# Start of a fused FFT and MLP kernel: batch 0's x loaded ahead of the small loads, its first transform cut into row halves, weight pieces split earlier

## The chip, the cores and the metric

The kernel runs on one core of a Trainium2 chip. The metric is the device time of one execution in microseconds; lower is better.

## The reference

```python
def _attn_ref(x, w_r, w_i, b_r, b_i):            # x: 8 batches of 3008 x 256
    X = np.fft.rfft(x, axis=1)
    Yr = Xr @ w_r - Xi @ w_i + b_r;  Yi = Xr @ w_i + Xi @ w_r + b_i
    Yr, Yi = (sign(Y) * max(|Y| - 0.01, 0) for Y in (Yr, Yi))
    return np.fft.irfft(Yr + 1j * Yi, n=3008, axis=1)
def _moe_ref(x, w_in, w_out):                     # 24064 x 256, w_in 256 x 2048
    h = x @ w_in
    return (h * np.cos(h)) @ w_out
```

`w_in` and `w_out` are stored as 64-bit floats.

## The kernel before

The FFT of 3008 = 64 x 47 points is done by matmuls. For batch 0 all of it stands in a prologue, in which nothing of the MLP runs yet. **Stage A** (`stage_a0`) is the transform of length 64: six tiles `x0` (128 x 1024, 512 KB each) come from memory, and each block of 128 columns of them is the stationary operand of a matmul that streams the 128 columns of `ff`. These 128 columns hold two 64-row transforms on the diagonal, so half of what is multiplied is zero. A float32 matmul is two instructions on TensorE; the stage has 48 matmuls, 96 instructions. Twelve PSUM banks are copied out to `a0`, ScalarE and VectorE in turn (L435). **Stage B** (`first()` in `stage_b`) transposes (`pq`, L542), transforms along 47 (`pb`, L642), mixes by the weights (`pw`, L664), shrinks, transposes back (`pt`) and transforms back (`pi`, L791). It is a generator; the prologue's loop counts its steps in `i`. Then `stage_c` transforms back along 64 (`pc`) and yields the first MLP tile, t=0 of batch 0, whose matmuls are `ph` (L939 to L941) and `po` (L921 to L925). The MLP's steps are in a fixed order, with later batches' transforms between them.

The **weight pieces** are beside that: 16 pieces of `w_in` and `w_out` come as raw words (`raw`, 512 KB each, issued by GpSimd, L257) and `split_f64` turns each into a high and a low part, with two ScalarE and seven VectorE instructions (L270 to L279, and L332 by `rest`). `W_AT` lists the steps `i` at which a piece enters the order; twelve pieces are split ahead of t=0 (`W_BEFORE`), four in its steps `W_LATE`. Raw loads from index `W_NEXT` on wait for the first `pc` matmul. `split_fourier_w` casts the Fourier weights `ws` to `wf` for later batches (ScalarE L233, VectorE L234). `bounds` prepares the clamp's limits from the biases `bb`; `sig` and `fi` serve the inverse transform; `iw`, `sgn`, `fq` serve later batches; `xt` are batch 1's first two x tiles.

`tc.issue_after(ins)` keeps what is issued under it behind `ins` in the planned order. Each engine runs its own queue in order. The planner sets the order of each queue from its own estimates.

Of the kernel before, what the change touches and what calls it, by code (L numbers as in the profile page):

```python
# [31 lines left out]
XP_BUFS = 6  # L32
W_AT = (8, 16, 24, 32, 40, 48, 56, 64, 74)
W_ORDER = tuple(range(16))
W_EARLY = 10
W_NEXT = 13
W_BEFORE = 12
W_LATE = (0, 3, 6, 9)
W_AHEAD = 3
# [139 lines left out]
def tile_body(ctx: ExitStack, tc, x, w_r, w_i, b_r, b_i, w_in, w_out,  # L179
# [27 lines left out]
    def load_constants():  # L207
        with nc.allow_non_contiguous_dma(reason="bias"):
            for r, bsrc in enumerate((b_r, b_i)):
                nc.gpsimd.dma_start(bb[:, r, :], bsrc.rearrange("(c p) -> p c", p=128))  # L210
        ws["sig"] = pool["pro"].tile([96, 32], F32, name="sig", bufs=1)
        nc.gpsimd.dma_start(ws["sig"], c_sig)
        nc.gpsimd.dma_start(fi[0], c_if)
        ws["minus"] = wk.tile([128, 64], F32, tag="xe", name="minus", bufs=2)
        nc.gpsimd.tensor_scalar(out=ws["minus"], in0=ff[:, 256:], scalar1=-1.0, scalar2=None, op0=ALU.mult)

    def load_split_constants():
        nc.gpsimd.dma_start(iw, c_iw)
        nc.gpsimd.dma_start(sgn.rearrange("p s k -> p (s k)"), c_sgn.bitcast(BF16))
        nc.gpsimd.memset(odd, 0.0)  # L220
# [34 lines left out]
    def load_f64(raw, src, behind_it="x0"):  # L255
        with tc.issue_after(mark[behind_it].ins):
            ins = nc.gpsimd.dma_start(raw if len(src.shape) == 2 else raw.rearrange("p (f e) -> p f e", f=2), src)  # L257
            if behind_it == "pc":
                behind(ins, mark["pc"].ins, "first tile")
        return raw  # L260

    def split_f64(k, hi, lo, raw):
# [16 lines left out]
        nc.scalar.copy(hi, a)  # L279
        rest(lo, a, hi)  # L280

# [134 lines left out]
    def stage_a0():  # L416

        a0[0] = pool["a0"].tile([128, 2, 24, 128], F32, name="a0", bufs=1)
        xs = []
        for c in range(6):  # L420
            xs.append(pool["pro"].tile([128, 1024], F32, tag="xp", name="x0", bufs=XP_BUFS))
            nc.sync.dma_start(xs[c], x[0, :, 1024 * c:1024 * (c + 1)])
        load_f0(0)
        load_f0(1)
        load_fourier_w()
        load_f0(2)
        landed("x0", xs[5][:, :1])
        for n in range(12):
            p = fps("pa")
            for c in range(2):  # L430
                for i in range(2):
                    o, k = 256 * c + 128 * i, 512 * (n % 2) + 256 * i + 128 * c
                    mm(p[:, o:o + 128], xs[n // 2][:, k:k + 128], ff[:, :128], start=o == 0, stop=o == 384,
                       skip_group_check=True)
            mark["dve"] = mark["a0", n % 2] = (nc.vector.tensor_copy if n % 2 else nc.scalar.copy)(  # L435
                a0[0][:, :, 2 * n:2 * n + 2], p.rearrange("p (c i k) -> p c i k", c=2, i=2))

    def stage_a(b):
# [3 lines left out]
        def load(c):  # L442
            if c < 6:
                ld[c] = wk.tile([128, 2, 2, 256], F32, tag="xt", name="xt", bufs=2)
                with tc.issue_after(mark["f0", 2].ins) if b == 1 else ExitStack():
                    ins = (nc.sync if b == 1 else nc.gpsimd).dma_start(
                        ld[c].rearrange("p i g d -> p (i g d)"), x[b, :, 1024 * c:1024 * (c + 1)])
# [84 lines left out]
    def stage_b(b):  # L532
# [15 lines left out]
        def load(q):  # L548
            if b and q < 4:
                fq = wk.tile([128, 512], F32, tag="fq", name="fq", bufs=2)  # L550
                with tc.issue_after(mark["x0"].ins) if b == 1 else ExitStack():
                    loads = [nc.gpsimd.dma_start(fq, c_fq[:, 512 * q:512 * q + 512])]
# [321 lines left out]
    def stage_c(b, t):  # L874
# [23 lines left out]
        for g in range(2):  # L898
            pv = p[g].rearrange("p (c i m) -> p c i m", c=2, i=4)
            thv, tlv = (a.rearrange("p c (i g m) -> p g c i m", i=4, g=2)[:, g] for a in (th, tl))  # L900
            nc.scalar.copy(thv, pv)  # L901
            ins = nc.vector.tensor_tensor(out=tlv, in0=pv, in1=thv.bitcast(F32), op=ALU.subtract)  # L902
            drained(p[g], ins)
        if first:
            with tc.issue_after(ins.ins):
                split_fourier_w()
            mark["yf"] = ins
# [62 lines left out]
    with ExitStack() as first:  # L970
# [13 lines left out]
        fi[0] = pool["pro"].tile([96, 2, 96], F32, name="fi", bufs=1)  # L984
        stage_a0()
        load_constants()
        stages["a"] = stage_a(1)
        side_a = stages["a"].alone()
        next(side_a)
        split = 0  # L990
        stages[0] = stage_b(0)
        for i, _ in enumerate(stages[0].first()):
            if i == 0:
                load_pieces(2)
                with tc.issue_after(mark["x0"].ins):
                    load_split_constants()
            if i == 4:
                with tc.issue_after(mark["a0", 1].ins):
                    sum_fourier_w()
                    bounds()  # L1000
            if split < len(W_AT) and i >= W_AT[split]:
                next(mw)
                split += 1
        for _ in side_a:
            pass
        last, mark["yf"] = mark["yf"], mark["yf0"]
        next(mw)
        mark["yf"] = last
        for _ in range(len(W_AT) + 1, W_BEFORE):
            next(mw)  # L1010
# [101 lines left out]
```

## Time and profile before

| | us |
|---|---|
| median of 3 runs | 2602.94 (2596.9 to 2603.41) |
| the profiled execution | 2602.17 |
| its span | 2600.4 |
| TensorE busy | 2561.9 |
| granted TensorE clock, mean share | 0.995 |

The span runs from the first to the last instruction of the profiled execution; 1.8 us of its time lie around it. Times inside are counted from the start of the span. TensorE's busy share is of instructions in flight, not of its peak.

### The profile page before, as it was taken

How to read it: one execution, taken by the hardware profiler on the slowest of the kernel's cores; microseconds unless marked ns; L12 is line 12 of the kernel's file. 1: busy time of each engine (PE TensorE's matmuls, PEld its weight loads, DVE VectorE, ACT ScalarE, POOL GpSimd, SP SyncE). 2: the span in 40 equal slices, each digit the busy share in tenths (PEclk: the TensorE clock that was granted, in tenths of full speed). 3: DMA queues.
4: the chain of work that ended last, by engine and by line, in shares of the span. 5: the costliest groups of instructions: out<-in, count | busy, mean ns of one | idle time of the engine just before them, and what ended most of it. 6: DMA issues, size and time to landing. Idle time of an engine off the chain costs nothing.

```text
span 2600.4 us, 42935 instructions
## 1 busy us (share of the span) xinstructions
PE 2561.9 (99%) x15961; PEld 2070.0 (80%) x15961; DVE 1937.1 (74%) x3089; ACT 1629.6 (63%) x3003; POOL 977.5 (38%) x946
## 2 busy tenths in 40 slices
PE   8899999999999999999999999999999999999999
PEld 7478778877788777887788877887778888888888
DVE  5887776877768787687777877678776778766665
ACT  5665556655675666655666666666666666666666
POOL 2025452444325443344533455234432333322222
PEclk9999999999999999999999999999999999999999
DMA  7546434444333444254432644235433344210000
GB/s 233 160 116 160 143 107 112 113 143 130 104 95 100 140 131 117 81 141 121 142 93 83 160 139 121 78 103 146 135 105 100 84 111 119 62 46 24 17 25 16
DMA packets 172953, 283.11 MB, mean 109 GB/s; under 512 B 15608, under 2 KB 114200, under 8 KB 169160
## 3 DMA queue, kind: packets, MB, share of 16 engines
q1 hardware_dynamic: 161896, 243.78, 33.3%
q0 software_dynamic: 10112, 35.53, 4.4%
q8 instruction: 126, 2.06, 0.3%
q10 hardware_dynamic: 736, 1.05, 0.1%
q14 instruction: 83, 0.68, 0.1%
HBM read 149.76 MB, written 130.55 MB: 108 GB/s over the span
## 4 chain that ended last, share of the span: by engine, by line
PE 87%; DVE 6%; DMA 3%; ACT 2%; issue 1%; SPq 0%; POOL 0%; DVEq 0%; ACTq 0%; POOLq 0%
PE ph L939 12%; PE po L921 12%; PE ph L940 12%; PE ph L941 12%; PE po L925 12%; PE po L922 12%; PE pw L668 2%; PE pw L669 2%; PE pw L670 2%; PE pc L381 1%; PE pb L381 1%; PE pw L664 1%; DVE u L952 1%; DVE u L949 1%; DVE Xl L332 1%
## 5 line engine op out<-in xcount | busy, mean ns | idle before, releaser
L329 POOL TENSOR_TENSOR gl<-u,gh 128x512 fp32r<-128x512 f32 (+1 forms) x384 | 500.7, 1304 | 1125.6 <-ACT gh L954 942.6
L951 ACT ACTIVATE u<-u 128x512 f32<-128x512 f32 (+1 forms) x768 | 478.0, 623 | 385.7 <-DVE u L949 384.8
L952 DVE TENSOR_TENSOR u<-ph,u 128x512 f32<-128x512 f32 (+1 forms) x768 | 518.0, 675 | 236.3 <-ACT u L951 225.2
L949 DVE SCALAR_TENSOR_TENSOR u<-ph,u 128x512 f32<-128x512 f32 (+1 forms) x768 | 513.4, 671 | 239.5 <-ACT u L948 238.6
L954 ACT CAST gh<-u 128x512 fp32r<-128x512 f32 (+1 forms) x768 | 467.8, 609 | 250.3 <-DVE u L952 245.1
L921 PE MATMUL po<-gh,wout 128*128 128x512 f32 (+1 forms) x1536 | 600.0, 391 | 14.6 <-ACT gh L954 14.6
L948 ACT ACTIVATE u<-ph 128x512 int32<-128x512 f32 (+1 forms) x768 | 447.9, 586 | 263.3 <-PE ph L941 256.2
L939 PE MATMUL ph<-xTh,win 128*128 128x512 f32 (+1 forms) x1536 | 604.0, 393 | 1.8 <-ACT xTh L901 1.6
L940 PE MATMUL ph<-xTl,win 128*128 128x512 f32 (+1 forms) x1536 | 596.5, 388 | 0.1
L941 PE MATMUL ph<-xTh,win 128*128 128x512 f32 (+1 forms) x1536 | 595.7, 388 | 0.0
L922 PE MATMUL po<-gh,wout 128*128 128x512 f32 (+1 forms) x1536 | 593.7, 387 | 0.0
L925 PE MATMUL po<-gl,wout 128*128 128x512 f32 (+1 forms) x1536 | 476.5, 388 | 0.0
L939 PEld LDWEIGHTS ph<-xTh,win 128*128 128x128 f32 x1536 | 289.7, 189 | 90.7 <-issue 21.6
L921 PEld LDWEIGHTS po<-gh,wout 128*128 128x128 f32 x1536 | 288.6, 188 | 84.4 <-ACT gh L954 23.8
L332 DVE TENSOR_TENSOR gl<-u,gh 128x512 fp32r<-128x512 f32 (+1 forms) x384 | 294.3, 767 | 79.9 <-ACT gh L954 73.3
L925 PEld LDWEIGHTS po<-gl,wout 128*128 128x128 f32 x1536 | 287.5, 188 | 60.1 <-issue 4.9
L941 PEld LDWEIGHTS ph<-xTh,win 128*128 128x128 f32 x1536 | 289.8, 189 | 57.1
L940 PEld LDWEIGHTS ph<-xTl,win 128*128 128x128 f32 x1536 | 289.8, 189 | 50.9 <-DVE xTl L902 0.6
L922 PEld LDWEIGHTS po<-gh,wout 128*128 128x128 f32 x1536 | 288.8, 188 | 50.7
L332 DVE TENSOR_TENSOR Xl<-z,Xh 128x384 fp32r<-128x384 f32 x112 | 109.9, 1009 | 11.9 <-ACT Xh L602 8.9
L668 PE MATMUL pw<-Xh,wf 128*128 128x384 f32 x336 | 115.2, 343 | 1.8 <-ACT Xh L617 1.8
L717 POOL TENSOR_TENSOR odd<-st 128x184 f32<-128x184 f32 (+1 forms) x112 | 68.4, 613 | 123.2 <-DVE st L694 102.5
(123 smaller groups left out, 2448.1 us busy)
## 6 DMA issues: line engine op xcount, KB each, us to landing
scrF<-at SPq DMA_DIRECT2D x28, 1024.0 KB
z<-scrF SPq DMA_DIRECT2D x112, 256.0 KB
scrT<-tr SPq DMA_DIRECT2D x56, 512.0 KB
y<-scrT SPq DMA_DIRECT2D x112, 256.0 KB
bt<-scr SPq DMA_DIRECT2D x94, 256.0 KB
scr<-ao SPq DMA_DIRECT2D x84, 256.0 KB
scr<-bo SPq DMA_DIRECT2D x224, 96.0 KB
out_dram<-ob SPq DMA_DIRECT2D x80, 256.0 KB
```

The lines of the kernel that those rows point to most:

```text
L329: return nc.gpsimd.tensor_tensor(out=lo, in0=x, in1=hi.bitcast(F32), op=ALU.subtract)
L921: mm(po[e][:, :n], wo[0][:, 0, f, es], gh[:, :n], start=f == 0, stop=False)
L922: mm(po[e][:, :n], wo[0][:, 1, f, es], gh[:, :n], start=False, stop=False)
L925: mm(po[e][:, :n], wo[0][:, 0, f, es], gl[:, :n], start=False, stop=f == NFC - 1)
L939: mm(h, win[:, 0, c, fs], th[:, c, :n], start=c == 0, stop=False)
L940: mm(h, win[:, 0, c, fs], tl[:, c, :n], start=False, stop=False)
L941: ins = mm(h, win[:, 1, c, fs], th[:, c, :n], start=False, stop=c == 1)
L948: nc.scalar.activation(k[:, :n], h, AF.Identity, bias=0.25, scale=1.0 / TWO_PI)
L949: nc.vector.scalar_tensor_tensor(out=u[:, :n], in0=h, scalar=1.0 / TWO_PI, in1=k[:, :n], op0=ALU.mult, op1=ALU.subtract)
L951: nc.scalar.activation(u[:, :n], u[:, :n], AF.Sin, bias=HALF_PI, scale=TWO_PI)
L952: product = nc.vector.tensor_tensor(out=u[:, :n], in0=h, in1=u[:, :n], op=ALU.mult)
L954: step = [nc.scalar.copy(gh[:, :n], u[:, :n])]
```

## The change

Stage A of batch 0 does each block as two matmuls, one on rows 0 to 63 and one on rows 64 to 127, each streaming 64 columns of `ff` into a bank of its own. GpSimd's small loads (`bb`, `sig`, `fi`) come behind the arrival of x and the first two raw loads. `iw`, `sgn`, `fq` and `xt` are issued later. The cast of the Fourier weights is also held behind ScalarE's cast of the first `pc`. Ten pieces instead of nine stand in the loop, at other steps, and thirteen instead of twelve ahead of t=0.

```diff
-W_AT = (8, 16, 24, 32, 40, 48, 56, 64, 74)
+W_AT = (6, 10, 15, 24, 33, 43, 53, 63, 73, 80)
-W_NEXT = 13
-W_BEFORE = 12
-W_LATE = (0, 3, 6, 9)
+W_NEXT = 14
+W_BEFORE = 13
+W_LATE = (0, 4, 8)
...
     def load_constants():
-        with nc.allow_non_contiguous_dma(reason="bias"):
-            for r, bsrc in enumerate((b_r, b_i)):
-                nc.gpsimd.dma_start(bb[:, r, :], bsrc.rearrange("(c p) -> p c", p=128))
         ws["sig"] = pool["pro"].tile([96, 32], F32, name="sig", bufs=1)
-        nc.gpsimd.dma_start(ws["sig"], c_sig)
-        nc.gpsimd.dma_start(fi[0], c_if)
+        with tc.issue_after(mark["x0"].ins):
+            with nc.allow_non_contiguous_dma(reason="bias"):
+                for r, bsrc in enumerate((b_r, b_i)):
+                    nc.gpsimd.dma_start(bb[:, r, :], bsrc.rearrange("(c p) -> p c", p=128))
+            nc.gpsimd.dma_start(ws["sig"], c_sig)
+            nc.gpsimd.dma_start(fi[0], c_if)
...
-        for n in range(12):
-            p = fps("pa")
+        for m in range(6):
+            p = [fps("pa") for _ in range(2)]
             for c in range(2):
-                for i in range(2):
-                    o, k = 256 * c + 128 * i, 512 * (n % 2) + 256 * i + 128 * c
-                    mm(p[:, o:o + 128], xs[n // 2][:, k:k + 128], ff[:, :128], start=o == 0, stop=o == 384,
-                       skip_group_check=True)
+                for i in range(4):
+                    for g in range(2):
+                        o, k = 256 * c + 64 * i, 256 * i + 128 * c
+                        mm(p[g][:, o:o + 64], xs[m][64 * g:64 * g + 64, k:k + 128],
+                           ff[64 * g:64 * g + 64, :128].rearrange("p (r g s) -> p g r s", r=2, g=2)[:, g],
+                           start=o == 0, stop=o == 448, skip_group_check=True)
+            for g in range(2):
+                mark["dve"] = mark["a0", g] = (nc.vector.tensor_copy if g else nc.scalar.copy)(
...
-                with tc.issue_after(mark["f0", 2].ins) if b == 1 else ExitStack():
+                with tc.issue_after(mark["f0", 5].ins) if b == 1 else ExitStack():
...
-                with tc.issue_after(mark["x0"].ins) if b == 1 else ExitStack():
+                with tc.issue_after(mark["iw"].ins) if b == 1 else ExitStack():
                     loads = [nc.gpsimd.dma_start(fq, c_fq[:, 512 * q:512 * q + 512])]
...
-            nc.scalar.copy(thv, pv)
+            cast = nc.scalar.copy(thv, pv)
...
-            with tc.issue_after(ins.ins):
+            with tc.issue_after(ins.ins), tc.issue_after(cast.ins):
                 split_fourier_w()
...
         stage_a0()
+        load_pieces(2)
         load_constants()
         stages["a"] = stage_a(1)
         side_a = stages["a"].alone()
-        next(side_a)
...
-            if i == 0:
-                load_pieces(2)
-                with tc.issue_after(mark["x0"].ins):
+            if i == 36:
+                with tc.issue_after(mark["raw"].ins):
                     load_split_constants()
+            if i == 30:
+                next(side_a)
             if i == 4:
                 with tc.issue_after(mark["a0", 1].ins):
                     sum_fourier_w()
+            if i == 11:
+                with tc.issue_after(mark["rest"].ins):
                     bounds()
...
-        last, mark["yf"] = mark["yf"], mark["yf0"]
-        next(mw)
-        mark["yf"] = last
-        for _ in range(len(W_AT) + 1, W_BEFORE):
+        for _ in range(len(W_AT), W_BEFORE):
             next(mw)
```

## Rows read from the trace of the kernel before

**Rows 1.** The page: TensorE's busy time, and the chain that ended last, by engine.
```profile
PE 2561.9 (99%) x15961; PEld 2070.0 (80%) x15961; DVE 1937.1 (74%) x3089; ACT 1629.6 (63%) x3003; POOL 977.5 (38%) x946
...
PE 87%; DVE 6%; DMA 3%; ACT 2%; issue 1%; SPq 0%; POOL 0%; DVEq 0%; ACTq 0%; POOLq 0%
```
**Rows 2.** Timeline of stage A's end: start, duration, instruction, idle before and releaser.
```profile
6.61 12.39 PE L433 MATMUL pa<-ff,x 128*128 128x128 f32 x96 [1.81 <-DMA ff<-in_dram]
...
16.33 0.19 POOL L409 COPY seen<-x 128x1 f32<-128x1 f32 x1 [9.30 <-DMA x<-in_dram]
...
19.03 0.69 DVE L435 COPY a<-pa 128x512 f32<-128x512 f32 x1 [1.09 <-PE pa L433]
19.10 0.62 ACT L233 CAST wf<-ws 128x512 fp32r<-128x512 f32 x1 [5.74 <-DMA ws<-in_dram]
19.62 1.55 ACT L435 COPY a<-pa 128x512 f32<-128x512 f32 x3
...
21.27 1.09 PE L542 MATMUL pq<-ident,a 128*96 128x128 f32 x8 [2.28 <-ACT a L435]
```
**Rows 3.** Windows, L433 alone: length, PE and PEld busy, clock, DMA, GB/s.
```profile
6.60:9.50 2.90, 2.89 (x13) 2.89 (x14) 1.00 0.82 184
...
9.70:15.30 5.60, 5.60 (x53) 5.60 (x52) 1.00 1.03 308
```
**Rows 4.** Windows of all engines: PE, PEld, DVE, ACT, POOL busy, granted clock.
```profile
23.20:26.60 3.40, 3.40 (x17) 3.32 (x16) 0.00 (x0) 2.01 (x5) 1.51 (x3) 0.50 1.03 393
26.60:30.00 3.40, 3.40 (x30) 3.40 (x30) 0.00 (x0) 2.75 (x7) 1.14 (x3) 0.99 1.02 389
...
40.00:50.00 10.00, 8.69 (x51) 6.45 (x50) 7.81 (x16) 6.04 (x14) 0.53 (x1) 1.00 0.25 81
```
**Rows 5.** Timeline at two moments, 44.56 and 44.64: weight loads begun so far.
```profile
44.51 0.19 PEld L664 LDWEIGHTS pw<-Xf,ws 128*128 128x128 f32 x1 [0.48 <-ACT Xf L644]
...
44.51 0.30 PEld L664 LDWEIGHTS pw<-Xf,ws 128*128 128x128 f32 x2 [0.48 <-ACT Xf L644]
```
**Rows 6.** Windows, `pc` alone: 64-row, 64-column matmuls on four array quarters.
```profile
112.50:113.70 1.20, 1.20 (x62) 1.11 (x62) 0.00 (x0) 0.00 (x0) 1.00 0.00 0
```
**Rows 7.** Groups by line, 30.8 to 112.7 us, VectorE: count, busy us, mean ns.
```profile
L274 DVE SCALAR_TENSOR_TENSOR wa<-raw,wa 128x512 uint32<-128x512 uint32 x12 | 8.3, 690 | 0.3
...
L332 DVE TENSOR_TENSOR win<-wa,win 128x512 fp32r<-128x512 f32 x8 | 5.5, 688 | 1.8 <-ACT win L279 1.6
...
L272 DVE TENSOR_SCALAR wa<-wa 128x512 uint32<-128x512 uint32 x12 | 5.1, 425 | 0.3
```
**Rows 8.** Windows, all engines, from the first piece to the last before t=0.
```profile
30.80:112.70 81.90, 77.12 (x404) 47.34 (x406) 70.10 (x134) 54.36 (x117) 3.73 (x6) 1.00 0.45 139
```
**Rows 9.** The chain that ended last, in order of time: start, us, what.
```profile
101.46 0.69 DVE yf L775
...
111.96 0.70 DVE wout L332
...
120.13 11.57 DMA bt<-scr
```
**Rows 10.** Timeline: first users of what the change loads or computes later.
```profile
34.85 0.48 DVE L692 TENSOR_SCALAR cl<-st,blo,bhi 128x384 f32<-128x384 f32 x1
...
43.04 0.27 PE L770 MATMUL pt<-ident,st 128*96 128x128 f32 x1
...
49.66 1.07 PE L791 MATMUL pi<-yf,fi 96*96 96x256 f32 x4 [1.04 <-ACT yf L783]
...
96.70 0.64 PE L371 MATMUL pa<-xt,ff 64*64 64x512 f32 x1
```
**Rows 11.** DMA: 119 to 132 us in all; issues to 140 us, KB, us to landing.
```profile
DMA packets 3110, 4.52 MB, mean 347 GB/s; under 512 B 214, under 2 KB 2608, under 8 KB 3108
...
raw<-in_dram POOLq DMA_DIRECT2D x16, 512.0 KB, 7.9
...
fi<-in_dram POOLq DMA_DIRECT2D x1, 72.0 KB, 8.4
```

More of the change, by code (lines that the diff above doesn't have):

```diff
@@ L217, in load_split_constants @@
     def load_split_constants():
-        nc.gpsimd.dma_start(iw, c_iw)
+        mark["iw"] = nc.gpsimd.dma_start(iw, c_iw)
         nc.gpsimd.dma_start(sgn.rearrange("p s k -> p (s k)"), c_sgn.bitcast(BF16))
@@ L256, in load_f64 @@
         with tc.issue_after(mark[behind_it].ins):
-            ins = nc.gpsimd.dma_start(raw if len(src.shape) == 2 else raw.rearrange("p (f e) -> p f e", f=2), src)
+            mark["raw"] = ins = nc.gpsimd.dma_start(raw if len(src.shape) == 2 else raw.rearrange("p (f e) -> p f e", f=2), src)
             if behind_it == "pc":
@@ L279, in split_f64 @@
         nc.scalar.copy(hi, a)
-        rest(lo, a, hi)
+        mark["rest"] = rest(lo, a, hi)
     def words(k):
@@ L427, in stage_a0 @@
         landed("x0", xs[5][:, :1])
-        for n in range(12):
-            p = fps("pa")
+        for m in range(6):
+            p = [fps("pa") for _ in range(2)]
             for c in range(2):
-                for i in range(2):
-                    o, k = 256 * c + 128 * i, 512 * (n % 2) + 256 * i + 128 * c
-                    mm(p[:, o:o + 128], xs[n // 2][:, k:k + 128], ff[:, :128], start=o == 0, stop=o == 384,
-                       skip_group_check=True)
-            mark["dve"] = mark["a0", n % 2] = (nc.vector.tensor_copy if n % 2 else nc.scalar.copy)(
-                a0[0][:, :, 2 * n:2 * n + 2], p.rearrange("p (c i k) -> p c i k", c=2, i=2))
+                for i in range(4):
[6 more added lines that the diff above has]
+                mark["dve"] = mark["a0", g] = (nc.vector.tensor_copy if g else nc.scalar.copy)(
+                    a0[0][:, :, 4 * m:4 * m + 4].rearrange("p c i (r g s) -> p c (i r) g s", r=2, g=2)[:, :, :, g],
+                    p[g].rearrange("p (c i s) -> p c i s", c=2, s=32))
     def stage_a(b):
```

## The prediction, as it was put on record

> **What bounds the kernel now.** I read the page first, then the windows and the timeline of the prologue, then the chain. TensorE is busy nearly the whole span and holds 87% of the chain that ended last [rows 1]. From about 133 us on the kernel is a row of MLP matmuls that the change does not touch. So the change can only shift the moment at which this row starts, and what it can win is what TensorE loses before that. Three losses can be seen there. First, after the last stage A matmul TensorE stands still for 2.28 us until the first transpose at 21.27, and the releaser is ScalarE's copy of `a0` [rows 2]. That copy is late because a cast of `wf`, which nothing needs yet, stood ahead of it in ScalarE's queue, waited 5.74 us for `ws`, and ran at 19.10. Second, soon after this pause the granted clock falls to 0.50 (the lower level, 1.2 GHz) from 23.2 to 26.6: 17 matmuls start there, 30 in the next stretch of that length [rows 4]. Third, near the end the chain goes through VectorE's pieces and then through 11.57 us of waiting for `bt` of the second tile, up to 131.7 [rows 9]. Between these VectorE is busy 70.1 of 81.9 us [rows 8], and TensorE waits little.
>
> Stage A itself is not held by x: it waits for `ff` alone and then runs 12.39 us without a pause [rows 2]. Its first part ran at half rate, 13 instructions in 2.9 us (0.22 each) against 53 in 5.6 (0.106 each) [rows 3], although the clock column prints 1.00 in both: the first stretch is at the lower level, after matmuls on an idle tile and a pause.
>
> **Stage A by row halves.** Ninety-six instructions become 192, in 96 pairs on the two halves of the array's rows. Streaming gets cheaper: a pair streams 64 columns where an instruction streamed 128. The nearest row is `pc`, 64 columns against 64-column weights on four quarters: 62 in 1.20 us, 0.077 for four [rows 6]. So 96 pairs would need at most 96 x 0.077 = 7.4 us; half of the present step gives 96 x 0.053 = 5.1. But each pair still loads 128 columns of x as weights. From an idle array, two loads of 128 columns were under way for 0.30 us in all where one takes 0.19 [rows 5]: a second load begins 0.11 after the first. Ninety-six times 0.11 is 10.6 us, the same as now at full clock (96 x 0.106 = 10.2). Loads of different quarters run side by side, since four fit into 0.077 [rows 6], so I count the two halves' loads as side by side too. If they were not, 192 x 0.11 = 21.1. I take the load as the bound, because rows 5 has the very width that stays: stage A takes 12.4 us as before and ends at 19.0. Change 0; ends -7.3 and +8.7.
>
> The Trainium skill speaks to the same point: TensorE: Matmul & The Clock Gate, section "LDWEIGHTS (loading the stationary operand)", says that a load's time goes by its columns and not by its rows, and gives a figure that makes 107 ns of 128 columns. By that rule an estimate of the stage is 96 x 0.107 = 10.3 us, no gain from halving rows; the row of this trace agrees (0.11).
>
> **The cast held back.** Three casts of 0.62 us leave ScalarE's start, and they come back behind the first `pc`, where ScalarE and TensorE go through the MLP's start; there they are off the chain or cost under 1 us each. Without them the copies follow the matmuls. The last one is VectorE's, 19.03 + 0.69 = 19.72 [rows 2]. The transposes then start at about 19.85 instead of 21.27: -1.4 us.
>
> **The clock.** The pause shrinks from 2.28 to 0.85 us. A pause of 1.04 us, before `pi` at 49.66 [rows 10], stands in a stretch with clock 1.00 [rows 4], and 0.85 is nearer to that than to 2.28. So I expect no fall: 3.4 x (1 - 17/30) = 1.5 us come back. Ends 0 and -1.5.
>
> **x ahead of the small loads.** In the stretch from 6.6 to 9.5, DMA moves 184 GB/s against 308 later [rows 3]. If all of that dip is due to `bb`, `sig` and `fi`, x arrives 2.9 x (308 - 184) / 308 = 1.2 us before 16.33. As stage A waits for TensorE and not for x, this gives nothing directly; raw words come that much sooner. The delayed loads have slack: issued by about 20 and landing at most 8.4 us later [rows 11], against first uses at 34.85 (limits from `bb`) and 49.66 (`fi`) [rows 10]. `xt`, issued near step 30 of 80-odd and so by the middle of the prologue, is used at 96.70; `iw`, `sgn` and `fq` serve batch 1 and later, behind t=0. All 0. If `bb` took as long as the `bt` load (11.57) it would still be in time.
>
> **bounds behind two pieces.** `bounds` now waits on VectorE for the second piece. A piece is four VectorE instructions of 0.69 us and three of 0.42 [rows 7] (there L274 stands for L277 and L278 too, and L272 for L271 and L276), 4.0 us; two are 8.1. The first piece began at 30.8 [rows 8]; it now stands two steps of `i` sooner (a step is two transposes and four `pb`, 6 x 3.4 / 30 = 0.7 us by rows 4) in an order that is 2.9 us sooner, so at about 26.5, and its raw words, issued behind x near 15.5, land 7.9 later [rows 11], at 23.4. The two pieces end at 34.6, some 3.5 us after the shifted first clamp would run. The first reader of what is clamped is the transpose at 43.04 [rows 10], 8 us later, and evictions of `pw` are not behind the clamp. 0; more than 8 us of delay would reach TensorE.
>
> **One more piece ahead of t=0.** VectorE gets 4.0 us more before t=0, 74 in all. It can begin 4 us sooner and has 11.8 idle us in the window of rows 8, so it fits. Three whole pieces now follow the last `yf`: 12.1 us, against 10.5 from 101.46 + 0.69 to 111.96 + 0.70 [rows 9]. With the whole prologue 2.9 us sooner the last ends 1.6 later by its own start, still before the first tile's `pc` has been cast. 0, at worst +1.6. The fourteenth raw load now waits for a buffer that the eleventh piece frees, so 512 KB move while the first tile's result is stored and reloaded: at 347 GB/s 1.5 us of all engines [rows 11]. I take +0.5 (0 to +1.5).
>
> **One raw load fewer behind the first `pc`.** The same 1.5 us of transfer leave the stretch in which `bt` waits [rows 9, 11]. I take -0.7 (0 to -1.5), since part of the wait is the stores ahead of it in SP's queue.
>
> **Sum.** 0 - 1.4 - 1.5 + 0.5 - 0.7 = -3.1 us. Against the profiled execution's own 2602.17 us this is 2599.1. The median of the runs shown is 0.8 above that execution, and the runs lie 6.5 us apart.
>
> **Rivals.**
> *Streaming sets the pace.* Were two loads hidden behind the halves' streaming, stage A would go at 5.1 to 7.4 us of TensorE, or as x arrives. With x at 15.1 and the last tile's 16 pairs (1.2 us) it ends at 16.4, 2.6 sooner: 2596.5; with x no limit and 7.4 us, 5.0 sooner: 2594.1. For it: rows 6. Against it: rows 5. TensorEngine Tiling (Array Packing) in the Trainium skill, section "Theoretical Speedup", names up to twice the speed for dimensions of 64 or less, which would be this case; no row here shows it for 128-column loads.
>
> *The clock stays low in stage A (the other side).* If loads set the pace, the array streams only half of the time, 0.053 of 0.11 us. The trace has fallen to 0.50 after a stretch half empty [rows 2, 4]. If TensorE then runs all of stage A at the lower level, 96 x 0.22 = 21.1 us, it ends at 27.7 instead of 19.0: +8.7 - 1.4 + 0.5 - 0.7 = +7.1, 2609.3, with the clock term lost as well. It decides from the point where the stage takes 3.1 us longer than 12.4, 0.16 per pair; with the lower level in about half of it the time is near 2604. Loads that run one after the other would come to the same 2609.
>
> *The start is won and lost again on VectorE.* If the last `yf` is paced by VectorE and not by TensorE, 4.0 us more work there eat the 2.9 gained: 2602. For it: 70.1 of 81.9 us busy; against it: 11.8 idle.
>
> **How the numbers follow.** My forecast (gain 1 to 5 us) 0.45, streaming 0.22, low clock 0.18, VectorE 0.15. A change of 0.3% is 7.8 us, about what a measurement of this kernel can tell from no change: under 2595.1 or over 2610.7 by the median shown. Only streaming reaches the first in good part (0.14), and 0.04 of the forecast's tail with `bt`'s wait gone wholly; only low clock reaches the second (0.06), with 0.01 for a mishap in the queues. Faster 0.18, same 0.75, slower 0.07. The range holds the first three cases and the milder half of the low clock: 2593 to 2607. The forecast's own is 2597 to 2601.5.
>
> **What would show it.** Right: 192 L433-like matmuls in about 10 to 12.5 us with loads 0.11 apart, no L233 cast before the first `pc`, a first `pq` near 19.9, clock 1.00 from 10 to 100 us, the last piece's end near 110, and `bt` of the second tile landing before 129. Wrong: stage A ending by 17 (streaming), or after 22 with matmuls 0.2 apart (clock); a first `pq` gained but the last piece before t=0 ending no sooner than 112.7 (VectorE or the raw load).

## The result, and the profile after

Four runs of each, on one chip: 2617.44 us after (2616.23 to 2619.25), 2602.93 before; ratio 1.0062 (interval 1.0048 to 1.0076). The change makes the kernel 14.5 us or 0.6% slower, where 2599.1 was forecast. The profiled execution took 2619.25 us, its span 2617.5, which is 17.1 above that of before.

The page after, busy time and the chain:

```profile
PE 2577.1 (98%) x16057; PEld 2080.9 (80%) x16057; DVE 1936.4 (74%) x3089; ACT 1629.4 (62%) x3003; POOL 977.2 (37%) x946
...
PE 84%; DVE 8%; ACT 3%; DMA 2%; issue 2%; POOL 1%; SPq 0%; ACTq 0%; DVEq 0%; POOLq 0%
```

TensorE is busy 15.2 us longer [rows 1], but a busy TensorE is not one at full speed. The timeline of the start shows where most of this is:

```profile
6.72 20.75 PE L435 MATMUL pa<-ff,x 64*128 64x64 f32 x192 [1.92 <-DMA ff<-in_dram]
...
11.80 0.19 POOL L410 COPY seen<-x 128x1 f32<-128x1 f32 x1 [4.67 <-DMA x<-in_dram]
...
27.54 0.69 DVE L439 COPY a<-pa 128x512 f32<-128x512 f32 x1 [2.72 <-PE pa L435]
...
28.38 1.92 PE L547 MATMUL pq<-ident,a 128*96 128x128 f32 x8 [0.91 <-DVE a L439]
```

Stage A has 192 matmuls, without a pause, and takes 20.75 us instead of 12.39 [rows 2]. The x tiles are there at 11.80, 4.5 us sooner, and wait for TensorE. No cast of `wf` stands ahead of the copies any more, and the first `pq` follows 0.91 us behind the last matmul instead of 2.28. The windows of L435 alone show the pace:

```profile
6.80:9.80 3.00, 3.00 (x30) 3.00 (x30) 1.00 1.02 412
9.80:15.40 5.60, 5.60 (x56) 5.60 (x54) 1.00 0.99 296
23.00:26.00 3.00, 3.00 (x32) 3.00 (x32) 1.00 1.03 421
```

Thirty instructions start in 3 us at the beginning and 32 at the end. Before, 13 in 2.9 us turned into 53 in 5.6 [rows 3]; here the step up never comes. The clock column prints 1.00 where the record of the clock has not begun. The mean durations tell the level, in the groups of the stage by form:

```profile
L435 PE MATMUL pa<-ff,x 64*128 64x64 f32 x192 | 20.7, 418 | 1.9 <-DMA ff<-in_dram 1.9
L435 PEld LDWEIGHTS pa<-ff,x 64*128 64x128 f32 x192 | 20.6, 330 | 2.6 <-DMA ff<-in_dram 2.6
```

A load takes 330 ns where the shortest row of before has 190 [rows 5]. The two matmuls of a pair start together, and a pair takes 20.75 / 96 = 0.216 us. The clock rises only in stage B, as the windows of all engines show: 15 matmuls in 3 us, then 27 of the same kinds.

```profile
31.30:34.30 3.00, 3.00 (x15) 2.93 (x15) 0.00 (x0) 1.43 (x4) 0.00 (x0) 1.00 0.06 20
34.50:37.50 3.00, 3.00 (x27) 3.00 (x27) 0.18 (x1) 2.60 (x7) 0.00 (x0) 1.00 0.27 74
```

By milestones of the two timelines, "after" is late by (us): first `pq` 7.1; first `pi` 7.7; last `pi` of batch 0 10.5; first `pc` 11.7; first `pb` of batch 1 8.4; first `pi` of batch 1 9.6; end of the span 17.1. So there are two losses of nearly one size: 7 to 8 us in stage A, and 7.4 us behind 270 us, in the MLP part, where the diff changes nothing. Between the two, 4.0 us are lost up to the first `pc`, 3.4 come back, since the second tile's `bt` is no longer waited for [rows 9], and 1.2 go up to the first `pi` of batch 1. The 7.4 us are of the two profiled executions; by the medians, 14.5 us apart, 4.9 are left for the MLP part.

### The profile page after: what moved, and what is told of

It reads as the page before. It is cut to its first block, busy times and chain, and to the rows that moved or that the text cites. A ratio compares the mean times of both kernels' runs of the same rounds, so it can differ in the third digit from the quotient of the medians.

```text
span 2617.5 us, 43130 instructions
## 1 busy us (share of the span) xinstructions
PE 2577.1 (98%) x16057; PEld 2080.9 (80%) x16057; DVE 1936.4 (74%) x3089; ACT 1629.4 (62%) x3003; POOL 977.2 (37%) x946
## 4 chain that ended last, share of the span: by engine, by line
PE 84%; DVE 8%; ACT 3%; DMA 2%; issue 2%; POOL 1%; SPq 0%; ACTq 0%; DVEq 0%; POOLq 0%
PE ph L944 12%; PE po L926 12%; PE ph L945 12%; PE ph L946 11%; PE po L927 11%; PE po L930 11%; PE pw L673 2%; PE pw L674 2%; PE pw L675 2%; DVE u L957 1%; PE pc L382 1%; DVE u L954 1%; PE pb L382 1%; DVE Xl L333 1%; PE pw L669 1%
## 5 line engine op out<-in xcount | busy, mean ns | idle before, releaser
L926 PE MATMUL po<-gh,wout 128*128 128x512 f32 (+1 forms) x1536 | 601.3, 392 | 17.3 <-ACT gh L959 17.1
L944 PEld LDWEIGHTS ph<-xTh,win 128*128 128x128 f32 x1536 | 289.6, 189 | 92.3 <-issue 22.4
```

The source lines that it names most:

```text
L926: mm(po[e][:, :n], wo[0][:, 0, f, es], gh[:, :n], start=f == 0, stop=False)
L944: mm(h, win[:, 0, c, fs], th[:, c, :n], start=c == 0, stop=False)
```

## The experiments

Eighteen kernels were run; "before" is the kernel before on the same chip. In the table, times in the last four columns are of the profiled execution: starts of the first `pq`, the first `pc` and the first `pi` of batch 1, and the time from the latter to the end of the span. "Moved" is counted from the traces: how many instructions of VectorE and ScalarE, behind the first 190 us of before, have to be put elsewhere to turn the kernel's order into that of before (of some 5600; another way of counting gives up to 3 fewer).

| kernel | us (before) | ratio, interval | pq | pc | pi, b1 | to the end | moved |
|---|---|---|---|---|---|---|---|
| before | | | 21.3 | 111.4 | 260.1 | 2340.3 | 0 |
| after | 2617.4 (2602.9) | 1.0048–1.0076 | 28.4 | 123.1 | 269.7 | 2347.8 | 36 |
| e1 full rows | 2605.7 (2601.4) | 1.0005–1.0024 | 20.3 | 111.4 | 258.8 | 2347.7 | 59 |
| e2 halves alone | 2613.0 (2601.4) | 1.0028–1.0058 | 29.3 | 120.6 | 267.4 | 2346.3 | 45 |
| e3 warm 13 | 2604.6 (2601.4) | 1.0003–1.0022 | 18.6 | 111.2 | 258.2 | 2343.2 | 24 |
| e4 quarters | 2604.4 (2601.4) | 1.0000–1.0021 | 21.9 | 116.5 | 261.9 | 2342.6 | 42 |
| e5 cast held | 2599.5 (2599.8) | 0.9991–1.0009 | 20.2 | 109.5 | 258.0 | 2340.2 | 11 |
| e6 start alone | 2598.8 (2599.8) | 0.9988–1.0007 | 20.4 | 108.8 | 257.3 | 2344.8 | 11 |
| e7 pieces alone | 2610.4 (2599.8) | 1.0023–1.0050 | 21.4 | 115.8 | 261.8 | 2348.5 | 56 |
| e8 start, warm 13 | 2601.4 (2599.8) | 0.9995–1.0014 | 18.6 | 107.0 | 254.1 | 2345.0 | 53 |
| e9 late raw | 2607.7 (2599.7) | 1.0016–1.0034 | 20.6 | 111.0 | 260.1 | 2348.6 | 59 |
| e10 twelve pieces | 2608.1 (2599.7) | 1.0019–1.0036 | 18.4 | 109.0 | 257.0 | 2348.0 | 59 |
| e11 quarters, warm 13 | 2612.0 (2599.7) | 1.0022–1.0050 | 21.4 | 113.8 | 260.6 | 2349.3 | 56 |
| e12 twelve, warm 13 | 2602.2 (2599.7) | 0.9996–1.0014 | 18.5 | 109.5 | 256.2 | 2344.1 | 39 |
| e13 before, warm 13 | 2606.9 (2600.1) | 1.0009–1.0031 | 21.1 | 112.5 | 260.8 | 2345.8 | 66 |
| e14 start, warm 9 | 2600.4 (2600.1) | 0.9992–1.0011 | 20.6 | 109.0 | 257.7 | 2341.7 | 19 |
| e15 before, warm 10 | 2603.9 (2600.1) | 1.0009–1.0027 | 20.6 | 109.3 | 257.8 | 2344.3 | 45 |
| e16 twelve, warm 9 | 2600.0 (2600.1) | 0.9989–1.0008 | 20.6 | 111.3 | 260.2 | 2337.4 | 20 |
| e17 after, warm 16 | 2601.1 (2600.7) | 0.9993–1.0011 | 18.8 | 111.3 | 256.7 | 2340.9 | 12 |
| e18 full rows, warm 9 | 2598.3 (2600.7) | 0.9980–0.9999 | 20.5 | 112.5 | 259.1 | 2340.0 | 20 |

Only one execution of each kernel was profiled. e6's took 2603.9, 5.1 more than its median; that is in its "to the end". The others lie within 2.8 us of their kernels' medians.

### The row halves and the clock (e1 to e4, e11)

The theory: each pair loads 128 columns of weights and streams 64, so loads set the pace, and at that rhythm the clock does not rise. The rivals: the two halves' loads run one after the other at full clock (the same 0.22 per pair), or it is another part of the change.

e1 is the changed kernel with stage A's old loop; e2 is the kernel before with nothing but the new loop.

> The changed kernel with the one edit of stage A taken back (128-row matmuls that stream 128 columns again), all else as changed. Theory A (row halves leave the array streaming half the time, the clock stays at its lower level through stage A, and that is most of the loss): stage A takes 12.4 us again instead of 20.8, the first transpose comes near 19.9 instead of 28.4, and the time falls by 8 to 10 us to about 2608; with the clock up at the start of stage B as well up to 11, 2606. Theory B (the loss sits in the pieces' new places and the start is beside the point): the first transpose comes 8 us sooner, but the first MLP matmul gains under 4 us, and the time stays above 2613.

> The kernel before with the row halves in stage A as its only edit. Theory A: stage A takes 20.5 to 21 us from 6.6, the first transpose comes near 28, some 7 us later than in the kernel before, and the time rises by 6 to 8 us to about 2610. Theory B: the later start is taken up by idle time of VectorE behind it, and the time stays within 3 us of 2603.

Timelines of TensorE, of e1 and then of e2:

```profile
6.79 12.61 PE L434 MATMUL pa<-ff,x 128*128 128x128 f32 x96 [2.01 <-DMA ff<-in_dram]
20.28 0.98 PE L543 MATMUL pq<-ident,a 128*96 128x128 f32 x7 [0.88 <-DVE a L436]
```

```profile
6.86 13.92 PE L434 MATMUL pa<-ff,x 64*128 64x64 f32 x128 [2.06 <-DMA ff<-in_dram]
21.34 7.09 PE L434 MATMUL pa<-ff,x 64*128 64x64 f32 x64 [0.56 <-ACT a L438]
29.34 1.92 PE L546 MATMUL pq<-ident,a 128*96 128x128 f32 x8 [0.91 <-DVE a L438]
```

The loop alone brings the slow stage (first `pq` at 29.34) and 11.6 us, more than either theory had; 7.3 of them are there at the first `pi` of batch 1. Without it the changed kernel is 4.3 us above before instead of 14.5. So the rest of the change is not the gain of 3.1 that was forecast either; that is for the next two sections.

e3 tells the clock from loads one after the other; it leaves the halves and only warms TensorE longer ahead of them:

```diff
-WARM = 7
+WARM = 13
```

> The changed kernel with 13 instead of 7 matmuls on an idle tile ahead of stage A, so that TensorE is busy without a pause from 1.4 to about 7 us. If loads of 128 columns set the pace of a pair (theory A): at the higher level a pair takes 0.11 us; where the clock has risen ahead of stage A it either stays up and the stage takes 10.5 to 11 us, or falls back to the lower level in the stage because the array streams only half the time, and it takes 16 to 20. If streaming sets the pace: a pair takes 0.06 at the higher level and the stage waits for x, ending near 13.5. If the two halves' loads go one after the other: 0.21 per pair at the higher level too. Time: 2606 to 2610 if the clock stays up, about 2615 if it falls back.

```profile
6.72 10.94 PE L435 MATMUL pa<-ff,x 64*128 64x64 f32 x192 [0.28 <-DMA ff<-in_dram]
18.57 1.69 PE L547 MATMUL pq<-ident,a 128*96 128x128 f32 x8 [0.91 <-DVE a L439]
```

With 13 idle matmuls and the pause ahead of the stage cut from 1.92 to 0.28 us the clock is high from the first matmul (the trace's clock record begins at 5.2 us and stands at 1.00 up to 18.9; in the changed kernel it begins at 34.4), and stage A takes 10.94 us, 0.114 per pair. So the halves' loads do run side by side, and a pair costs one load at either level: 0.114 and 0.216. The Trainium skill says in TensorE: Matmul & The Clock Gate, section "LDWEIGHTS (loading the stationary operand)", that a load goes by columns and not by rows; the trace agrees (64 rows 0.114, 128 rows 0.106 [rows 3]). Its figure for 128 columns, 107 ns, holds here at the higher level only: at the lower one it was 0.216.

The pause alone doesn't decide at which level the stage begins. With 7 idle matmuls it was the higher one in e5, e7 and e10, although TensorE paused as long; the timelines of e5 and e10:

```profile
7.01 5.62 PE L433 MATMUL pa<-ff,x 128*128 128x128 f32 x48 [2.21 <-DMA ff<-in_dram]
```

```profile
6.51 10.98 PE L434 MATMUL pa<-ff,x 128*128 128x128 f32 x96 [1.71 <-DMA ff<-in_dram]
```

With 9 or 10 it was the lower one in all four kernels (pauses of 0.74 to 1.36 us), with 13 or 16 the higher one in all six. What else decides is not shown; so e10's early first `pq` (18.4) is not a gain of its edit. The four runs of the changed kernel lie within 3 us, which leaves no room for a stage A 10 us shorter in some of them.

e4 takes the load away as the bound: the weights are cut into halves of columns too, 384 matmuls in groups of four on the array's quarters.

```diff
-                    for g in range(2):
-                        o, k = 256 * c + 64 * i, 256 * i + 128 * c
-                        mm(p[g][:, o:o + 64], xs[m][64 * g:64 * g + 64, k:k + 128],
+                    for v in range(2):
+                        for g in range(2):
+                            o, k = 256 * c + 64 * i, 256 * i + 128 * c + 64 * v
+                            mm(p[g][64 * v:64 * v + 64, o:o + 64], xs[m][64 * g:64 * g + 64, k:k + 64],
```

> The changed kernel with stage A cut once more, into quarters of the array: 64 rows by 64 columns of x as weights, 64 columns streamed, four matmuls side by side, 384 instructions. Theory A: a load now has as many columns as are streamed, so the array streams nearly all the time; the clock rises some 3 us after the start as in the kernel before, four matmuls take 0.11 to 0.12 us at the lower level and 0.06 at the higher, the stage takes 7 to 8 us and ends near 14 (x lands at 11.8), the first transpose comes near 14.5, 14 us sooner than in the changed kernel, and the time falls by 9 to 14 us to 2603 to 2608. If it is the number of instructions that costs (issue), the stage takes 20 us or more again.

Windows of its stage A matmuls, and the timeline:

```profile
6.70:9.70 3.00, 3.00 (x112) 3.00 (x116) 1.00 1.02 416
10.00:11.70 1.70, 1.70 (x103) 1.57 (x96) 1.00 1.06 349
14.80:17.40 2.60, 2.60 (x97) 2.60 (x100) 0.50 0.97 251
```

```profile
6.66 5.04 PE L436 MATMUL pa<-ff,x 64*64 64x64 f32 x215 [1.87 <-DMA ff<-in_dram]
14.79 3.69 PE L436 MATMUL pa<-ff,x 64*64 64x64 f32 x127 [3.08 <-issue]
19.57 1.44 PE L436 MATMUL pa<-ff,x 64*64 64x64 f32 x42 [1.09 <-issue]
```

Four matmuls take 0.107 us at the lower level, half of what a pair of halves took for the same work, and the clock does rise, near 10.4, and four take 0.066 (103 in 1.70). Then TensorE stands still for 3.08 us with nothing shown that it waits for, the clock falls to 0.50, and the gain is gone. e11 is e4 with 13 idle matmuls.

> The changed kernel with stage A in 64 x 64 quarters (as in e4) and 13 matmuls on the idle tile instead of 7. In e4 the clock rose at 10.3, four matmuls took 0.107 us at the lower and 0.059 at the higher level, and TensorE stood still twice, 3.08 and 1.09 us, with nothing awaited that the trace shows. If it comes in at the higher clock, 96 groups of four need 5.7 us and stage A waits for x (11.8) or for its own instructions. Theory I (TensorE runs out of instructions while x and the raw words fill the DMA queues): it stands still again for 3 us or more in all after some 200 matmuls, stage A ends at 16 to 19, the clock falls in the gap. Rival (the stalls came of the lower clock or of chance): stage A ends at 12.5 to 13.5 and the first pq stands near 14. Either way first pc no sooner than 108, as the pieces and the raw load set it, and a time within 3 us of e3's 2604.6.

```profile
6.80 3.30 PE L436 MATMUL pa<-ff,x 64*64 64x64 f32 x209 [0.74 <-DMA ff<-in_dram]
14.01 3.21 PE L436 MATMUL pa<-ff,x 64*64 64x64 f32 x127 [3.91 <-issue]
19.53 0.93 PE L436 MATMUL pa<-ff,x 64*64 64x64 f32 x48 [2.32 <-issue]
```

The clock is high at the start (209 matmuls in 3.30 us, 0.063 for four), and TensorE stands still again, after 209 instead of 215 of them and for 3.91 us. In both kernels the DMA engines are nearly always busy from 6 to 22 us. The trace shows the supply, too: one packet of 16 KB on the queue of instructions in each long pause, in the DMA views of e4 (11.7 to 14.8 us) and e11 (10.1 to 14.0):

```profile
q8 instruction: 1, 0.02, 2.4%
```

```profile
q8 instruction: 1, 0.02, 2.0%
```

These packets land at 13.27 and 12.56 us, the next ones at 18.13 and 18.12, and after each of the four TensorE goes on 1.4 to 1.5 us later. Between the two pauses run 127 matmuls and as many loads, in both kernels. So TensorE waited for instructions; whether they came so late because x and the raw words filled the DMA engines is not shown.

### The pieces, the late loads and the cast (e5 to e10)

e5 is the kernel before with the cast held back and nothing else. e6 is e1 with the pieces, `bounds` and the loop's end as before, so that the later loads and the cast are left. e7 is the kernel before with the pieces' new places and count alone. e8 is e6 with 13 idle matmuls. (The "Theory A" of these texts is that the pieces' new places cost the 4.3 us of e1.)

```diff
+            cast = nc.scalar.copy(thv, pv)
...
+            with tc.issue_after(ins.ins), tc.issue_after(cast.ins):
                 split_fourier_w()
```

> The kernel before with one edit: the three casts of wf held back behind the first pc. Theory A (the prediction's terms for the cast and the clock hold; the rest of the change lost them): first pq at 19.9 instead of 21.27, no stretch at the lower clock behind it, first pc 1.4 to 2.9 us before 111.4, time 1 to 3 us below before. Rival (VectorE's pieces set the first pc whatever the start does): first pq earlier, first pc at 111.4 again, time within 1 us of before, or above it by what the three casts cost behind the first pc (up to 2 us).

> The changed kernel with stage A's old form and with the pieces as they were (old W_AT, W_NEXT, W_BEFORE, W_LATE, bounds at its old place): what is left is the late small loads and the cast held back. Theory A (the pieces' new places cost the +4.3 us that the changed kernel with the old stage A has over before): first pc near 108.5, time 2 to 3 us below before. Rival (the late loads or the cast cost it): time 3 to 5 us above before, as with the pieces moved.

> The kernel before with the pieces' new places, their new count ahead of the first tile and bounds behind two of them, and nothing else of the change. Theory A (the pieces cost it): first pc 3 us or more after 111.4, time 4 to 8 us above before. Rival (the late loads and the cast cost it, or where the rows of later matmuls fall): time within 2 us of before.

> The kernel of e6 (late small loads, cast held back, old stage A, old pieces) with 13 matmuls on the idle tile instead of 7 ahead of x. If TensorE comes into stage A at the higher clock, the first 13 of the 96 instructions take 0.11 instead of 0.22 us each: 1.4 us less, stage A ends near 18.0 and the first pq stands at 18.9. Theory A: first pc near 107.5 and a time 3 to 4 us below before, below both kernels. Rival (VectorE's pieces or the raw loads set the first pc): first pc as in e6, no gain over e6.

e5 and e6 have their first `pc` 1.8 and 2.5 us sooner and are as fast as before. e7 is 10.6 us slower, so the pieces looked guilty. But its first `pi` of batch 1 is only 1.8 late, and 8.1 of its 9.9 us of span are lost behind it; and e8, which begins batch 1 5.9 us sooner than before, is 1.6 above it. Up to the first `pc` the pieces have two prices. From the first `pi` to the last took 55.1 us before and in e5, e6 and e8, and 56.3 in e1 and e7, where TensorE waits 2.6 instead of 1.1 us for VectorE's `yf`. In the changed kernel, e9 and e10 it took 57.6 to 57.9: there the clock also falls behind this wait, as the windows of the changed kernel show (length; PE, PEld, DVE, ACT, POOL busy; clock):

```profile
109.50:112.90 3.40, 3.40 (x10) 1.80 (x9) 1.97 (x6) 1.42 (x3) 0.00 (x0) 0.50 0.22 63
```

The fourteenth raw load holds up the first tile; the timeline of e1's ScalarE and then the DMA issues near the first `pc` of e1 and of e6 (KB, us to landing):

```profile
111.22 0.68 ACT L271 ACTIVATE wa<-raw 128x512 f32<-128x512 f32 x1 [2.55 <-DMA raw<-in_dram]
```

```profile
raw<-in_dram POOLq DMA_DIRECT2D x3, 512.0 KB, 5.9
...
bt<-scr POOLq DMA_DIRECT2D x2, 128.0 KB, 5.6
```

```profile
raw<-in_dram POOLq DMA_DIRECT2D x2, 512.0 KB, 6.2
...
bt<-scr POOLq DMA_DIRECT2D x2, 128.0 KB, 3.4
```

It runs beside the reload of `bt`, which takes 5.6 us instead of 3.4, and ScalarE waits 2.55 us for it. e9 and e10 take it away from e1: e9 puts the load behind `pc`, e10 also goes back to twelve pieces.

```diff
-W_NEXT = 14
-W_LATE = (0, 4, 8)
+W_NEXT = 13
+W_LATE = (3, 6, 9)      # e9; e10: W_BEFORE = 12, W_LATE = (0, 3, 6, 9)
```

> The changed kernel with stage A's old form (as in e1) and the fourteenth raw load behind the first pc (W_NEXT 13), split with the next two at steps 3, 6 and 9. In e1 this 512 KB load ran from 105.2 to 111.1 beside the reload of the first tile (bt took 5.6 us from issue to landing instead of 3.4) and ScalarE waited 2.55 us for it ahead of two copies. Theory R (that load is what the pieces' part costs): bt of the first tile lands in about 3.5 us, first pc near 109.3 instead of 111.4, no wait of ScalarE for raw before it, time 2 to 4 us below e1's 2605.7. Rival V (thirteen pieces on VectorE are the cost): first pc within 0.5 us of 111.4, time within 1 us of e1.

> The changed kernel with stage A's old form, the pieces at their new steps, but twelve instead of thirteen ahead of the first tile, the fourteenth raw load behind the first pc (W_BEFORE 12, W_NEXT 13, W_LATE 0, 3, 6, 9 as before). Theory R and V both: first pc at 109 or sooner, time 1 to 3 us below before. Rival P (the early places delay the s chain on VectorE, whatever their count): last pi and first pc no sooner than in e1 (103.0, 111.4) and a time 2 us or more above before.

`bt` lands in 3.5 us again in e9, and from the last `pi` to the first `pc` it is 6.4 and 6.5 us instead of 8.4. Both kernels are 8 us above before all the same, e10 although its batch 1 begins 3.1 us sooner (stage A began there at the higher clock). Theory R is right on the load and wrong on the time. What is lost is lost in the MLP part, in kernels that there do the same work.

### The order of the queues behind (e12 to e18)

The traces show that a change in the start alters the planner's order in the MLP part: few instructions, but over all batches. The expectations speak of some 390 moved instructions of VectorE; that count came from a comparison which slid by a whole batch. Counted rightly (table) it is 5 to 34 for VectorE and 4 to 32 for ScalarE. GpSimd's order (1 to 9 instructions) and TensorE's move with them; the order of the DMA issues of SyncE's queue is the same in all. The rival: the pieces, or the early start itself, cost the time.

e12 is e10 with 13 idle matmuls, e16 e10 with 9. e13 and e15 are the kernel before with 13 and 10 and no other edit. e14 is e6 with 9, e17 the changed kernel with 16, e18 e1 with 9: counts at which the planner keeps or nearly keeps the orders of before. All are edits of one line, `WARM = 7`.

> The kernel of e10 with 13 matmuls on the idle tile instead of 7: the candidate with the early start and without the thirteenth piece. If the start's gain is carried to the first tile: last pi 1.4 us before that of e10, first pc 1 to 1.5 us sooner, the first batch 1 pb 5 us or more before that of the kernel before, and a time 2 to 5 us below before. Rival (what the start wins is given back in the MLP part, as in e8, where pb of batch 1 stood 6 us sooner and the time was not lower): time within 2 us of before.

> The kernel before with 13 matmuls on the idle tile instead of 7, and nothing else. The planner then sets the MLP part's orders anew (some 390 of 2843 instructions of VectorE stand elsewhere, as in e8). Theory O (the new order of VectorE and ScalarE in the MLP part costs 4 us or more): stage A ends 1.4 us sooner, pb of batch 1 stands no later than before, and the time is still 2 to 6 us above before. Rival (the order costs nothing, the losses of e1, e7, e9 and e10 come of the pieces): time 0 to 1.5 us below before.

> The kernel of e6 (late small loads, cast held back, old stage A and pieces) with 9 matmuls on the idle tile instead of 7; the orders of the MLP part stay those of before. Theory O: what the start wins is kept to the end: first pc 2.5 to 4 us before 111.4, time 1 to 4 us below before, no worse than e6. Rival (e8's loss came of the earlier start itself, which the MLP part gives back): time at before or up to 2 us above, as e8. The candidate that could beat both kernels.

> The kernel before with 10 matmuls on the idle tile. Here the planner moves more: twice as many instructions of ScalarE as in e13, and also a quarter of GpSimd's. Theory O: 2 us or more above before though the start is up to 1.4 us sooner. Rival: within 1.5 us of before or below it.

> The kernel of e10 (early pieces, twelve of them, late loads, cast held back; 8.4 us above before) with 9 matmuls on the idle tile: ScalarE's order in the MLP part is then nearly that of before, VectorE's is not. If ScalarE's order is what costs: time within 2 us of before. If VectorE's order costs, or the pieces themselves: 4 us or more above before.

> The changed kernel, row halves and all, with 16 matmuls on the idle tile instead of 7. The planner then gives VectorE, ScalarE and GpSimd nearly the orders of before in the MLP part (16 to 17 instructions stand elsewhere), and the last idle matmul ends at about 7, so that stage A begins at the higher clock. If both causes are right (the clock in stage A, the orders behind): stage A in 10.9 us, first pc near 111 as in e3, pi of batch 1 no later than 260, and from there to the end no longer than before: 2598 to 2602, 16 us below the changed kernel and 3 to 6 below e3, which has the clock but not the orders. Rival (the orders are not the cause): as e3, 3 to 5 us above before.

> The kernel of e1 (old stage A, all the rest of the change; 4.3 us above before) with 9 matmuls on the idle tile: ScalarE's order in the MLP part is nearly that of before (28 instructions stand elsewhere), VectorE's is not. If ScalarE's order is the cause: 3 to 5 us below e1, within 2 us of before, although the first pc stands where it stood. Rival (chance in e16, the pieces are the cause): as e1, 3 to 6 us above before.

e13 speaks most plainly against the pieces as the only cause: six more matmuls on an idle tile, batch 1 begun 0.7 us later than before, 66 instructions moved, 6.7 us slower (2.3 to 8.1 by the interval). e15 goes the same way (3.8 us slower though batch 1 begins 2.3 sooner). e16 has e10's pieces, begins batch 1 3.2 us later than e10 and is 8 us faster; e18 has e1's pieces and a first `pc` 1.1 us later than before, and is the fastest kernel here. e17, the changed kernel with stage A at the higher clock and nearly the orders of before, is at the time of before. e12 lies between (2.4 us above, 39 moved). In the column "to the end", the six kernels with at most 20 moved have 2337.4 to 2344.8, mean 2340.8, as before; the seven with over 50 have 2345.0 to 2349.3, mean 2347.6; the six between, with the changed kernel, 2344.7. The pauses of TensorE behind the first `pi` of batch 1, summed from the traces, go the same way: 18.8 us before, 19.3 to 21.1 in the six, 22.4 to 26.8 in the seven. So do the medians: their distance to before, less what is there at that `pi`, is 1.3, 8.4 and 4.6 us on average in the three groups. No run sets an order by itself, so that the order is the cause rests on this agreement and on e13 and e15.

e14's gain at the start (2.3 us) is not seen in its time, within 2.5 us. Nor are those of e5, e6 and e17 (2.0 to 3.3 us): all four keep nearly the order of before and end 1.0 us below to 0.5 above it. The rival that the MLP part gives back a gain of this size stays open.

Where it goes is seen in what TensorE waits for from 260 us on (us in total, times, longest), in e10 and then in e16; before it is 14.6, in e17 15.3, in the changed kernel 16.9:

```profile
PE po L922 <- ACT gh L955: 20.3, 13, 3.7
```

```profile
PE po L922 <- ACT gh L955: 13.9, 12, 2.7
```

One such place, VectorE's timeline, first in e10 and then in e16:

```profile
272.47 0.68 DVE L950 SCALAR_TENSOR_TENSOR u<-ph,u 128x512 f32<-128x512 f32 x1
273.07 0.43 DVE L726 STREAM_TRANSPOSE tr<-odd 128x256 f32<-128x256 f32 x1
273.43 0.65 DVE L950 SCALAR_TENSOR_TENSOR u<-ph,u 128x512 f32<-128x512 f32 x1
274.01 0.42 DVE L725 STREAM_TRANSPOSE tr<-st 128x256 f32<-128x256 f32 x1
274.36 0.65 DVE L953 TENSOR_TENSOR u<-ph,u 128x512 f32<-128x512 f32 x1
```

```profile
275.13 1.28 DVE L950 SCALAR_TENSOR_TENSOR u<-ph,u 128x512 f32<-128x512 f32 x2
276.33 0.43 DVE L726 STREAM_TRANSPOSE tr<-odd 128x256 f32<-128x256 f32 x1
276.68 0.65 DVE L953 TENSOR_TENSOR u<-ph,u 128x512 f32<-128x512 f32 x1
```

In e10 a second transpose for batch 1 stands between the two `u` of the MLP's chain, and the `gh` that TensorE waits for comes later: TensorE stands still for 3.62 us there and 2.71 in e16. The pause has a second price, in e10's windows (length; PE, PEld, DVE, ACT, POOL busy; clock):

```profile
272.10:275.70 3.60, 0.00 (x0) 0.00 (x0) 3.60 (x8) 1.92 (x4) 2.26 (x3) 0.92 0.00 0
275.70:282.40 6.70, 6.69 (x18) 5.53 (x19) 2.67 (x5) 3.30 (x7) 3.55 (x3) 0.53 0.56 186
```

The clock stays at the lower level for 6.7 us behind it. How long it does so is not told by the pause's length: by the clock records it was 3.4 us behind a pause of 3.72 us in e10 (at 335.9), 3.4 behind 2.71 before (at 275.2), and none behind 2.71 in e16. Over the whole MLP part of the changed kernel, all pauses of TensorE sum to 23.1 us against 18.8 before, and the lower level to 20.5 us against 13.7: 4.3 + 6.8 / 2 = 7.7 us, for the 7.4 that the milestones give. In e1 and e13 the lower level sums to no more than before, and the pauses make nearly all of the loss (6.3 us of 7.4, 4.9 of 5.5).

What stays open: which of the moved instructions matter. e16 and e18 speak for ScalarE's (13 moved, against 29 in e1 and e10), but VectorE's count falls with it (from about 29 to 7).

## Why the prediction was wrong, point by point

- **Stage A by row halves: "Change 0".** The step that failed first. Its bound was right: one load of 128 columns per pair, halves side by side. It multiplied by a price at the higher clock (0.11), and the pairs never got there: 0.216, stage end 27.46 instead of 19.0. The rival "the clock stays low in stage A" had this with its price (21.1 us, end at 27.7; measured 20.75 and 27.46) and got a chance of 0.18. In e4, the same work with loads of half the width, the clock did rise; what about the halves keeps it low is not shown. The rival "streaming" fell with e3.
- **"A row of MLP matmuls that the change does not touch", so that the change "can only shift the moment" of its start.** The step that failed second, and no rival stood for it. The order behind changed with the start, and 7.4 us were lost after the first `pi` of batch 1 (4.9 by the medians), in e13 5.5 without any other edit.
- **The cast held back, and the clock behind it.** Right at their place with full rows: first `pi` in e1 2.9 us sooner, as forecast; the pause is 0.88 us and no fall of the clock follows it with full rows. In the changed kernel the pause shrank as forecast, but the clock term was lost: the lower level held up to 34.4. With the halves at high clock the same 0.91 us pause is followed by a fall (e3, e17). In the time of the kernel little of it can be seen (e5: 0.3 us, within 2.3).
- **x ahead of the small loads.** Under-sized: x is there 4.5 us sooner, not 1.2. Two loads of `xt`, issued at 12.32 us before, also no longer run beside x, and no run tells them from `bb`, `sig` and `fi`. In the changed kernel these three still stand ahead of the raw loads (11.93 against 14.53), not behind the first two. It wins nothing, as said, where TensorE is the bound; where stage A begins at the higher clock with the old loads, it waits 0.6 and 0.9 us for x in e7 and e5, not in e13.
- **bounds and the late constants.** 0, as said: TensorE waits for none of them in the changed kernel. No run takes them alone.
- **One more piece ahead of t=0 (+0.5, at most +1.5).** Too small and partly the wrong mechanism. VectorE's pieces do hold up `yf`, which the rival on VectorE had at up to 2.9 us and the sum at 0: the stretch from the first to the last `pi` grew by 1.2 us (e1, e7), in the changed kernel with the fall of the clock by 2.8. The raw load delayed `bt` and the first `pc` by 1.8 in e1, 1.9 in e7 and 1.2 in the changed kernel: 3.0 and 4.0 up to the first `pc`. The twelfth piece ended at 120.6 in the changed kernel and the thirteenth at 126.2, behind the first `pc`, not near 110.
- **One raw load fewer behind `pc` (-0.7, at most -1.5).** Under-sized: 3.35 us of waiting for `bt` at the second tile were gone in the changed kernel. In the kernels with the fourteenth raw load ahead the wait there is under 1 us, with it behind 1.1 to 3.4.
- **The sum.** The forecast of 2599.1 was 18 us too low. Stage A's +8 and the order's +7.4 are the two missing terms; nearly without them (e17: the halves at high clock, the order close to that of before) the changed kernel has a span of 2597.6 in its profiled execution and a median 0.5 us above before, 14 us less than as it was made, each against before on its own chip. That is still not the gain of 3.1 us.

No version beats the kernel before by more than 0.1%. The nearest is e18, 2598.26 against 2600.66.

## What to carry to other kernels

Cutting rows does not make a stage cheaper whose weight loads set its pace, and where streaming shrinks beside the loads the price must be taken at both clock levels, with what TensorE did before the stage. Where a planner orders the queues, an edit at the start is an edit of everything behind it: compare the orders of the untouched part first, and test with a neutral edit (one more idle matmul) before a few us are put down to the edit itself. Where a few dozen instructions stood in another order, the loss here was as large as all that the start could win.

## What the runs showed of the hardware that was not expected

- In 20.75 us of unbroken work on two halves side by side TensorE's clock did not rise; with the clock high at the start it stayed high through all 10.94 us (e3).
- After the same 7 idle matmuls stage A began at the higher level in three kernels (pauses of 1.71 to 2.21 us) and at the lower in others (1.81 and 1.92 us).
- TensorE stood still for 3.08 and 3.91 us in a stage of 384 small matmuls, after some 210 of them, while DMA was full, and went on 1.4 to 1.5 us after a 16 KB packet of instructions had landed (e4, e11).
- A pause of 3.62 us in the MLP part was followed by 6.7 us at the lower level, so that this pause cost about twice its length (e10); one of 3.72 us was followed by 3.4.
